# A conditioned attention and feed-forward block: a new written-out order that keeps VectorE and GpSimd apart on their shared port, with a rearranged prologue and filler products

## The chip, the cores and the metric

The kernel runs on one core of a Trainium2 chip. The metric is device time in microseconds, the median of several executions. A profiled execution has a span of its own, from the first to the last instruction. Engines: TensorE (PE), VectorE (DVE), ScalarE (ACT), GpSimd (POOL), and SyncE (SP), which here only issues DMAs.

## The reference

Cut to what matters. There are 2048 tokens of width 448, 16 heads of 28, and 4 segments of 512 tokens. Everything is bf16 in DRAM.

```python
sa, ca, ga, sb, cb, gb = (silu(c) @ w_mod) split in six        # vectors 0..5
h = layernorm(x) * (1 + ca) + sa
x = x + ga * A(h)                  # A: attention with a memory
h = layernorm(x) * (1 + cb) + sb
x = x + gb * (sigmoid(h @ w_gate) * (h @ w_up)) @ w_down

# A, per segment s, per head; q, k, v = h @ wq, h @ wk, h @ wv
a_dot = softmax(q k^T * scale + causal mask) @ v
a_mem = (phi(q) @ M) / (phi(q) @ z + 1e-6)      # phi(t) = t + 1 if t > 0 else exp(t)
o = g * a_mem + (1 - g) * a_dot                 # g = sigmoid(beta)
M += phi(k)^T v ; z += sum phi(k)               # carried to the next segment
A = concat(o) @ wo
```

## The kernel before

The work is tiled by segment (512 tokens, four tiles of 128 rows) and, in attention, by group of four heads (`hc`, four groups). Each segment goes through these stages:

- First norm (`ln1`, statistics L522 and L523 on DVE, reciprocal root L529 and L530 on POOL, `xn` L535 on DVE). For segment 0, TensorE transposes `xn` (L583), and DVE and ACT read the product from PSUM, scaled and shifted by vectors 0 and 1 (L594, L591). For the other segments a DMA transposes `xn` into `hT` (L545), and DVE and ACT scale and shift it in place (L558, L555).
- Projections (`proj`): q and k for each head group (L615, copied out by ACT at L623), v for each token tile (L636, copied at L640). The weights wq and wk are loaded into the buffer of `wd_sb` and copied into padded tiles (L448, L450).
- Attention for each head group: logits in three groups of key blocks (L695, four heads at once), exp on ACT (L704), causal mask on POOL (L710), the product with v (L718), transposition back (L725), normalization and gates (L741, L742, L756; from segment 1 on also the memory's part, L732, L762 and L764 on POOL), transposition again (L766, `oT`).
- Memory (`memory`): phi of k (L647 ACT, L648 and L650 DVE), a DMA transpose (L658), a product with v (L664), and the update (L671, L673, L677). phi of q goes the same way for L732.
- `wo_ln2`: the output product (L779), the residual (L783), the second norm (the same lines as the first), DMA transposes, modulation by vectors 3 and 4.
- `ffn`: fourteen chunks of 128 of the hidden width, each a gate and an up product (L799), tanh (L804), and a combination on DVE (L809); then the down product in three parts of its chunks (L822), the residual (L828), and the store (L830).

Vectors 2 and 5 are not applied to activations. POOL multiplies them into the weights: wo (four instructions, L506) and wd (fourteen, L508). Vectors come from products of silu(c) with w_mod, as columns (L417, read out at L426 and L424) or spread over all partitions (L434, L437). The w_mod columns of vectors 2, 3 and 4, and 5 are three loads into the feed-forward's `fT` buffers. Twenty products on zeros warm TensorE at the start (L836).

The order of all instructions is written out by a list scheduler in the program (class `Graph`): each piece of work is a node with an engine, a duration in ns, its predecessors, and a priority. The scheduler keeps a clock per engine, gives each engine the ready node of highest rank plus priority, hands out PSUM banks and ring buffers, and then emits the instructions in the order it found. It decides the order only; on the chip each engine runs its queue in order and waits on semaphores. `PRM` holds the priorities, and `pace` the earliest times of the head groups' logits:

```python
PRM = dict(T0=10000, STEP0=500.0, STEP=9700.0, lg=95000, ex=-30000, mask=127000, wo=9000, tanh=53500, up=85000,
           f=89500, dn=-507800, phi=8000, t=22000, ln1=-55000, mem=-86000, pj=-6000, ot=331000)
...
def pace(i):
    return PRM["T0"] + PRM["STEP0"] * min(i, NHC) + PRM["STEP"] * max(i - NHC, 0)
```

In this scheduler, DVE and POOL have separate clocks with no link between them, and a load may be issued once the modelled DMA queue is less than `BACKLOG` ns deep.

Of the kernel before, what the change touches and what calls it, by code (L numbers as in the profile page):

```python
# [9 lines left out]
U32 = mybir.dt.uint32  # L10
# [3 lines left out]
P = 128  # L14
# [3 lines left out]
BACKLOG = 1500  # L18


PRM = dict(T0=10000, STEP0=500.0, STEP=9700.0, lg=95000, ex=-30000, mask=127000, wo=9000, tanh=53500, up=85000,
           f=89500, dn=-507800, phi=8000, t=22000, ln1=-55000, mem=-86000, pj=-6000, ot=331000)
# [9 lines left out]
class Node:  # L32
    def __init__(self, eng, dur, fn, deps, take, use, lag, prio, release, mode, move):
        self.eng, self.dur, self.fn = eng, dur, fn
        self.deps = [d for d in deps if d is not None]
        self.take, self.use, self.lag, self.prio, self.release, self.mode = take, use, lag, prio, release, mode
        self.move = move
        self.start = self.end = None
        self.outs = []


class Graph:
# [15 lines left out]
    def add(self, eng, dur, fn, deps=(), take=(), use=(), lag=0, prio=0, release=0, mode=None, move=None):  # L58
        n = Node(eng, dur, fn, deps, take, use, lag, prio, release, mode, move)
# [7 lines left out]
    def ready_at(self, n):  # L67
        t = n.release
        if n.move is not None and n.move > 300:
            t = max(t, self.ring - BACKLOG)  # L70
# [9 lines left out]
    def place(self, n, t, narrow):  # L80

        got = []
        for s in n.take:
# [6 lines left out]
            else:  # L90
                c = [i for i, f in enumerate(free) if f <= t and (s, i) not in got]
# [9 lines left out]
                got.append(c[0])  # L101
        return got

    def run(self):
# [9 lines left out]
        self.ring = 0.0  # L114
        order, t, done = [], 0.0, 0
        while done < len(self.nodes):
            moved = False
            for e in ENGINES:
# [4 lines left out]
                for n in ready:  # L123
                    got = self.place(n, t, narrow)
# [5 lines left out]
                    for s, i in zip(n.take, got):  # L130
                        s.at = i
# [6 lines left out]
                    n.start = t  # L138
                    n.end = t + n.dur + extra
                    at[e] = n.end  # L140
                    if n.move is not None:
                        self.ring = max(self.ring, n.end) + n.move
                        n.lag = self.ring - n.end + LAND
                    avail[e].remove(n)
                    order.append(n)
                    done += 1
                    for s in {id(x): x for x in (*n.take, *n.use)}.values():
                        if all(u.end is not None for u in s.users):
                            f = max(u.end + (u.lag if u.move is not None else 0) for u in s.users) + 120
                            for w in range(s.width):  # L150
                                self.free[s.pool][s.at + w] = f
                    for o in n.outs:
# [8 lines left out]
            times += [r for e in ENGINES for n in avail[e] if (r := self.ready_at(n)) > t]  # L161
            times += [f for fs in self.free.values() for f in fs if t < f < float("inf")]
            assert times, "the graph cannot go on"
            t = min(times)
        for n in order:
            if n.fn is not None:
                n.fn()
        self.order = order
        Graph.last = self
# [3 lines left out]
def kernel(  # L173
# [35 lines left out]
    NWARM = 20  # L209
# [78 lines left out]
    BIG = 1e7  # L288

    def load(eng, dst, src, size, deps=(), prio=0, use=(), take=(), rate=230.0):  # L290
# [5 lines left out]
    l_c = load("SP", c_col[:], c.rearrange("o (p k) -> p (o k)", p=CP), 20000, prio=2 * BIG)  # L296
# [10 lines left out]
    def load_wm(engs, j0, nj, flat, prio, deps=()):  # L307
# [3 lines left out]
                   CP * h * nj * D * 2, prio=prio, deps=deps, rate=230.0 if nj == 1 else 300.0)  # L311
# [5 lines left out]
    def load_w(engs, dst, w, prio, deps=(), cuts=(0, 3)):  # L317

        n = w.shape[1]
        rate = 230.0 if n == D else 380.0  # L320
        a = w[0:3 * P, :].rearrange("(k p) n -> p k n", p=P)
        got = {}
        for i, (k0, k1) in enumerate(zip(cuts, cuts[1:])):
            x = load(engs[i], dst[:, k0:k1, :], a[:, k0:k1, :], (k1 - k0) * P * n * 2, prio=prio - i, deps=deps,
                     rate=rate)
            got.update((k, x) for k in range(k0, k1))
        got[3] = load(engs[-1], dst[0:KR, 3, :], w[3 * P:D, :], KR * n * 2, prio=prio - len(cuts), deps=deps, rate=rate)
# [3 lines left out]
    load_x("SP", 0, 1, 2 * BIG - 100)  # L331
    load_x("ACT", 1, 2, 2 * BIG - 100)
    load_x("SP", 2, 3, 2 * BIG - 200)
    load_x("ACT", 3, 4, 2 * BIG - 200)
    load_wm(("SP", "ACT"), 0, 2, pT_r[:].rearrange("p n h w -> p (n h w)"), 2 * BIG - 300)
    lq = load_w(("SP", "ACT", "ACT"), wq_st, A_wq, 2 * BIG - 400, cuts=(0, 2, 3))
    lk = load_w(("SP", "ACT", "ACT"), wk_st, A_wk, 2 * BIG - 500, cuts=(0, 2, 3))
    lv = load_w(("SP", "SP"), wv_sb, A_wv, BIG - 60)


# [15 lines left out]
    def pads_fn():  # L356
# [4 lines left out]
        nc.vector.memset(wv_sb[KR:P, 3, :], 0.0)  # L361

    n_wz = dve(200, lambda: nc.vector.memset(M_sb[:, 0:2, :], 0.0), prio=BIG)
    n_ident = pool_op(700, ident_fn, prio=BIG)
    n_pads = dve(1800, pads_fn, prio=BIG - 1)
# [4 lines left out]
    n_vpad = [pool_op(700, lambda i=i: vpad_fn(i), prio=BIG - 5) for i in range(NV)]  # L370
    n_wopad = pool_op(1500, lambda: nc.gpsimd.memset(wo_sb[:], 0.0), prio=BIG - 4)

    def gpad_fn():
        nc.gpsimd.memset(wg_sb[KR:P, 3, :], 0.0)
        nc.gpsimd.memset(wu_sb[KR:P, 3, :], 0.0)
        nc.gpsimd.memset(O_r[:, :, :, Dh:HP, :], 0.0)
    n_gpad = pool_op(3500, gpad_fn, prio=0, release=16000)


# [19 lines left out]
    n_bmask = dve(700, bmask2_fn, [pool_op(1700, bmask_fn, release=17000)])  # L399


    def silu_fn():
        nc.vector.tensor_scalar(th[:], th[:], 0.5, 0.5, op0=ALU.mult, op1=ALU.add)
        nc.vector.tensor_tensor(silu[:], th[:], c_col[:], ALU.mult)
    n_th = act(200, lambda: nc.scalar.activation(th[:], c_col[:], AF.Tanh, scale=0.5), [l_c], prio=BIG)
    n_silu = dve(400, silu_fn, [n_th], prio=BIG)
    n_sbc = dve(600, lambda: nc.vector.tensor_copy(
        silu_bc[:], silu[:].rearrange("p (k o) -> p k o", o=1).to_broadcast([CP, NK, P])), [n_silu])
    ROWS = (P, P, P, KR)

    def mod_cols(j, vi, prio):
# [15 lines left out]
        return n, dve(220, ev, [n], use=[b], prio=prio)  # L427
# [12 lines left out]
    mm1, n_ca = mod_cols(1, 1, BIG - 1)  # L440

    def padded(st, dst, loads, eng, prio):
        ns = []
        for k in range(NK):
            def fn(k=k, r=ROWS[k]):
# [3 lines left out]
                else:  # L449
                    (nc.vector if eng[k] == "DVE" else nc.gpsimd).tensor_copy(d, src)  # L450
            ns.append(add(eng[k], {"ACT": 600, "DVE": 400, "POOL": 1000}[eng[k]], fn, [n_pads, loads[k]],
                          prio=prio))
# [429 lines left out]
```

The softmax here doesn't subtract the row's maximum and nothing guards it: scores larger than these inputs give would overflow.

## Time and profile before

| | |
|---|---|
| time, median of 3 | 270.99 us (269.2 to 271.36) |
| span of the profiled execution | 266.6 us |
| PE, DVE, ACT, POOL busy | 245.8, 190.3, 158.0, 106.2 us |
| mean granted TensorE clock | 0.967 |
| L799, 448 matmuls | 117.5 us |
| L822, 224 matmuls | 45.2 us |
| L704, 48 exps | 76.6 us |
| L710, 64 masks | 42.2 us |
| L535, 32 of xn | 17.0 us (mean 568 ns) |
| L508, 14 scalings of wd | 15.3 us |
| HBM read, written | 10.67, 1.84 MB |

A busy time is the union of an engine's instructions. Matmuls overlap, so the mean duration of one (387 ns for 512 columns) is longer than the time from one to the next; the latter is read from the chain that ended last, or from the timeline. DMA rows give the time from the issue to the landing. A line number in a row is the line of the program.

### The profile page before, as it was taken

Reading aid. Unit: us, or ns where it says so; the run is one execution under the profiler, and the core shown is the slowest. Engines: PE = TensorE matmul, PEld = TensorE weight load, DVE = VectorE, ACT = ScalarE, POOL = GpSimd, SP = SyncE. Lnnn points to the kernel's source line nnn. Section 1 sums busy time; section 2 is a strip of 40 time slices with the busy share of each in tenths; the row PEclk is TensorE's granted clock in tenths of the full one; section 3 lists DMA queues with packets and bytes.
Section 4 is the critical chain, followed back from the end, with each engine's and each line's share of the span. In section 5 each row is a group of like instructions: output and inputs, shape, how many; then the busy total and the mean of one; then the engine's idle time right before and its main releaser. Section 6 shows DMA issues by size and latency. Waiting matters only on the chain.

```text
span 266.6 us, 4442 instructions
## 1 busy us (share of the span) xinstructions
PE 245.8 (92%) x1608; PEld 110.0 (41%) x1608; DVE 190.3 (71%) x392; ACT 158.0 (59%) x201; POOL 106.2 (40%) x168
## 2 busy tenths in 40 slices
PE   5799797788984999999999999999999999999994
PEld 1434333243331444444444444443444444444442
DVE  7679748839999999999968896488567833342334
ACT  0559898989885687986987564558521230331010
POOL 8648832447696564562434553006502300000000
PEclk9979899899996899999999999999999999999999
DMA  5999998761051010014011003000000131000103
GB/s 156 305 202 148 298 294 194 197 85 47 0 82 39 1 22 20 0 22 98 1 22 38 20 17 72 6 20 0 2 0 0 31 52 52 0 2 1 52 0 103
DMA packets 33245, 18.03 MB, mean 68 GB/s; under 512 B 22856, under 2 KB 32328, under 8 KB 33224
## 3 DMA queue, kind: packets, MB, share of 16 engines
q1 hardware_dynamic: 32248, 16.78, 29.1%
q10 hardware_dynamic: 976, 0.98, 1.4%
q8 instruction: 12, 0.20, 0.3%
q14 instruction: 9, 0.07, 0.1%
HBM read 10.67 MB, written 1.84 MB: 47 GB/s over the span
## 4 chain that ended last, share of the span: by engine, by line
PE 64%; DVE 3%; issue 1%; ACT 1%; DMA 1%; DVEq 0%
PE ps L799 37%; PE ps L822 15%; PE ps L779 4%; PE ps L695 3%; PE ps L615 2%; PE ps L718 2%; PE ps L732 1%; DVE ot L828 1%; DVE e L648 1%; ACT pT L704 1%; PE ps L664 1%; DMA out_dram<-ot 1%; DVE pq L650 1%; DVE hT L558 0%; DVE fT L809 0%
## 5 line engine op out<-in xcount | busy, mean ns | idle before, releaser
L704 ACT ACTIVATE pT<-ps 128x2048 bf16<-128x2048 f32 (+1 forms) x48 | 76.6, 1596 | 14.5 <-PE ps L695 13.6
L804 ACT ACTIVATE tt<-ps 128x512 f32<-128x512 f32 x56 | 33.4, 597 | 64.0 <-PE ps L799 62.6
L710 POOL TENSOR_SCALAR_AFFINE_SELECT pT<-pT 128x512 bf16<-128x512 bf16 x64 | 42.2, 673 | 60.9 <-ACT pT L704 60.7
L799 PE MATMUL ps<-hT,wg_sb 128*128 128x512 bf16 x224 | 59.0, 387 | 4.1 <-DVE hT L558 4.0
L809 DVE SCALAR_TENSOR_TENSOR fT<-tt,ps 128x512 bf16<-128x512 f32 x56 | 38.0, 682 | 32.2 <-PE ps L799 30.5
L799 PE MATMUL ps<-hT,wu_sb 128*128 128x512 bf16 x224 | 58.5, 384 | 0.0
L822 PE MATMUL ps<-wd_sb,fT 128*128 128x448 bf16 x224 | 45.2, 353 | 0.0
L799 PEld LDWEIGHTS <-wg_sb 128*128 128x128 bf16 x224 | 21.9, 99 | 30.6 <-DVE hT L558 4.3
L799 PEld LDWEIGHTS <-wu_sb 128*128 128x128 bf16 x224 | 21.1, 99 | 26.2 <-issue 2.6
L822 PEld LDWEIGHTS <-fT 128*128 128x128 bf16 x224 | 21.5, 98 | 20.0 <-issue 0.4
L522 DVE BATCH_NORM_STATS2 st<-x_sb 128x6 f32<-128x448 bf16 x32 | 19.5, 609 | 5.4 <-DMA x_sb<-in_A_x_dram 5.3
L764 POOL TENSOR_TENSOR O<-U 128x448 bf16<-128x448 f32 x12 | 13.8, 1150 | 21.2 <-DVE U L762 21.2
L695 PE MATMUL ps<-qT,kT 28*128 28x512 bf16 (+3 forms) x256 | 17.5, 306 | 3.7 <-ACT pT L704 3.1
L828 DVE TENSOR_TENSOR ot<-ps,x_sb 128x448 bf16<-128x448 f32 x16 | 9.9, 619 | 14.4 <-PE ps L822 13.0
L725 DVE STREAM_TRANSPOSE A<-ps 128x512 f32<-128x512 f32 x28 | 18.5, 691 | 1.8 <-PE ps L718 1.6
L615 PE MATMUL ps<-hT,wq_sb 128*128 128x512 bf16 x64 | 19.1, 427 | 0.3 <-DVE hT L594 0.3
L535 DVE TENSOR_SCALAR xn<-x_sb,mv,rs 128x448 bf16<-128x448 bf16 x32 | 17.0, 568 | 2.5 <-POOL rs L530 2.4
L615 PE MATMUL ps<-hT,wk_sb 128*128 128x512 bf16 x64 | 17.7, 402 | 0.0
L530 POOL TENSOR_TENSOR rs<-rs,mhalf 128x1 f32<-128x1 f32 (+1 forms) x23 | 15.2, 662 | 1.9
L650 DVE TENSOR_TENSOR pq<-e 128x512 bf16<-128x512 bf16 x24 | 14.3, 603 | 1.6 <-DVE e L648 0.5
L508 POOL TENSOR_TENSOR wd_sb<-wd_sb,rep 128x448 bf16<-128x448 bf16 x14 | 15.3, 1115 | 0.0
L779 PE MATMUL ps<-wo_sb,oT 128*128 128x448 bf16 x64 | 13.5, 353 | 1.4 <-DVE x_sb L783 1.4
(93 smaller groups left out, 261.8 us busy)
## 6 DMA issues: line engine op xcount, KB each, us to landing
out_dram<-ot SPq DMA_DIRECT2D x16, 112.0 KB, 1.7
x_sb<-in_A_x_dram SPq DMA_DIRECT2D x3, 448.0 KB, 7.1
wg_sb<-in_B_w_gate_dram SPq DMA_DIRECT2D x3, 448.0 KB, 6.2
wu_sb<-in_B_w_up_dram SPq DMA_DIRECT2D x3, 448.0 KB, 7.4
wd_sb<-in_B_w_down_dram SPq DMA_DIRECT2D x2, 448.0 KB
fT<-in_w_mod_dram SPq DMA_DIRECT2D x2, 392.0 KB, 7.3
fT<-in_w_mod_dram SPq DMA_DIRECT2D x1, 784.0 KB, 12.4
wd_sb<-in_B_w_down_dram SPq DMA_DIRECT2D x2, 336.0 KB
```

The source lines that it names most:

```text
L522: nc.vector.bn_stats(st_r[:, st.at, :], src)
L535: n = dve(330, lambda t=t, src=src, xn=xn: nc.vector.tensor_scalar(xn_r[:, xn.at, 0:D], src, mv_r[:, mv.at, t, 0:1], rs_r[:, mv.at, t:t + ...
L615: nc.tensor.matmul(pf(b), lhsT=w_sb[:, kc, hc * 4:(hc + 1) * 4, :].rearrange("p h e -> p (h e)"), rhs=hT_r[:, hT.at, kc, :], start=(kc == ...
L695: nc.tensor.matmul(ps[:, lg.at + hs, o:o + nq], lhsT=kT_r[r, k.at, hc, kb * P:(kb + 1) * P], rhs=qT_r[r, q.at, hc, kb * P:L], start=True, ...
L704: nc.scalar.activation(pT_r[:, pT.at, :, w0:w0 + wid], ps[:, lg.at:lg.at + 4, 0:wid], AF.Exp, scale=scale)
L710: nc.gpsimd.affine_select(out=blk, in_=blk, compare_op=ALU.is_ge, fill=0.0, base=0, pattern=[[0, 4], [1, P]], channel_multiplier=-1)
L725: nc.vector.transpose(A_r[:, A.at, i, :, :].rearrange("p b e -> p (b e)"), pf(b))
L779: nc.tensor.matmul(pf(b)[:, 0:D], lhsT=oT_r[:, oT.at, k, :].rearrange("p (q j) -> p j q", j=2)[:, t // 2, (t % 2) * P:(t % 2 + 1) * P], rh ...
L799: nc.tensor.matmul(pf(b), lhsT=w_sb[:, k, fs], rhs=hT_r[:, hT.at, k, :], start=(k == 0), stop=(k == NK - 1))
L804: a = act(500, lambda gp=gp, tt=tt: nc.scalar.activation(tt_r[:, tt.at, :], pf(gp), AF.Tanh, scale=0.5), [n1], use=[gp, tt], prio=PRM["tanh"])
L809: f = dve(605, lambda up=up, tt=tt, ft=ft: nc.vector.scalar_tensor_tensor(fT_r[:, ft.at, :], tt_r[:, tt.at, :], 1.0, pf(up), op0=ALU.add, ...
L822: nc.tensor.matmul(pf(b)[:, 0:D], lhsT=fT_r[:, fts[fc].at, t * P:(t + 1) * P], rhs=wd_sb[:, fc, :], start=(fc == 0), stop=(fc == NFC - 1))
```

## The change

The change aims at a shorter prologue and at fewer collisions between DVE and POOL.

1. The scheduler gets a common clock, `port`, for DVE and POOL work that is marked with `lock`: a marked node may not end before the port is free plus its own marked time, and if that would stall it for more than `PRM["stall"]` = 300 ns, other work is picked. Marked are the masks, xn, the in-place modulation on DVE, phi on DVE, the memory update's L677, the gate and normalization work, the weight scalings, and POOL's copies and several memsets. Durations are set lower for marked DVE work.
2. Loads: at most eight DMAs in flight instead of `BACKLOG`; other rates. w_mod's vectors 2 to 5 come in one load. wq and wk go through SP only. `c` comes first.
3. Segment 1's norm is turned on TensorE like segment 0's.
4. Prologue: an ACT operation of its own loads the function table early; the warm-up has 12 products; the head gates' operations and masks' constants come later; memsets of wo, wg and wu run as 32-bit words of half the number; the pads of `hT` are set once.
5. One of the fourteen wd scalings goes to DVE (`wdd=1`).
6. `fill`: after the order is found, dummy products on zeros or on `wq_sb` are put into TensorE's planned waits of more than 450 ns before 90 us, into a PSUM bank that is free there.
7. `PRM` has new values throughout.

In the order that results, eight dummies on zeros stand around the first transposes, and nine on `wq_sb` (three, one and five) between there and the first feed-forward product.

```diff
-BACKLOG = 1500
+LANES = 8
+FILL = 450
+PRM = dict(T0=5000, STEP0=500.0, STEP=10100.0, lg=69000, ex=40000, mask=-2000, wo=48000, tanh=24500, up=77000,
+           f=131500, dn=-486800, phi=-10000, t=8000, ln1_1=4000, ln1_2=-72000, ln1_3=-52000, mem=3000,
+           pj_0=3000, pj_1=-19000, pj_2=-15000, pj_3=37000, ot=399000, stall=300, wds=-22000, wos=145000,
+           wdd=1, mod=27000, a0=-62000, w0=3000)
...
+                    if n.lock is not None and self.port - t - n.lock > PRM["stall"]:
+                        continue
...
+                    if n.lock is not None:
+                        extra = max(0.0, self.port - t - n.lock)
                     n.end = t + n.dur + extra
+                    if n.lock is not None:
+                        self.port = n.end
...
+    def fill(self, until, fill):
+        pe = [n for n in self.order if n.eng == "PE"]
+        for a, b in zip(pe, pe[1:]):
+            one = 432 if a.end < 8000 else 216
+            n = int((b.start - a.end - FILL) / one)
+            if n <= 0 or a.end > until:
+                continue
...
-    NWARM = 20
+    NWARM = 12
...
-    lq = load_w(("SP", "ACT", "ACT"), wq_st, A_wq, 2 * BIG - 400, cuts=(0, 2, 3))
-    lk = load_w(("SP", "ACT", "ACT"), wk_st, A_wk, 2 * BIG - 500, cuts=(0, 2, 3))
+    lq = load_w(("SP",) * 3, wq_st, A_wq, 2 * BIG - 400 * MEG, cuts=(0, 2, 3))
+    lk = load_w(("SP",) * 3, wk_st, A_wk, 2 * BIG - 500 * MEG, cuts=(0, 2, 3))
...
+    n_act = act(1400, lambda: nc.scalar.activation(th[:], th[:], AF.Tanh), [n_th0], prio=2 * BIG - 350 * MEG)
...
-    n_wopad = pool_op(1500, lambda: nc.gpsimd.memset(wo_sb[:], 0.0), prio=BIG - 4)
+    n_wopad = pool_op(1000, lambda: nc.gpsimd.memset(wo_sb[:].rearrange("p c n -> p (c n)").bitcast(U32), 0),
+                      prio=BIG - 4 * MEG)
...
-    load_wm(("SP",), 2, 1, fT_flat[:, 2 * NK * D:], lp - 2)
+    load_wm(("SP",), 2, 4, fT_flat, lp - MEG * 2)
...
-    load_wm(("SP",), 3, 2, fT_flat, lp - 6)
...
-    load_wm(("SP",), 5, 1, fT_flat[:, 3 * NK * D:], 0)
...
-    n_coef = dve(1000, coef2_fn, [n_cf, n_hsel])
+    n_coef = dve(1000, coef2_fn, [n_cf, n_hsel], release=14000, lock=0)
...
+            (nc.gpsimd if on_pool else nc.vector).tensor_tensor(wd_sb[:, k, :], wd_sb[:, k, :], rep[:, 1, :], ALU.mult)
...
-        if s == 0:
-            ns = [layer_norms([x_sb[:, t, :]], [xl[t]], BIG - 2)[0] for t in range(TPS)]
+        if s < 2:
+            top = BIG - 2 * MEG if s == 0 else PRM["ln1_1"]
...
-                masks.append(pool_op(640, mask, [e], prio=PRM["mask"], use=[pT]))
+                masks.append(pool_op(610, mask, [e], prio=PRM["mask"] + a0, use=[pT], lock=0))
...
+    def dummy(i, n, at):
+        for _ in range(n):
+            if at < 12000:
+                nc.tensor.matmul(ps[:, i, :], lhsT=wz[:, 0:P], rhs=wz, start=True, stop=True)
+            else:
+                w = wq_sb[:, 0, :, :].rearrange("p h e -> p (h e)")
+                nc.tensor.matmul(ps[:, i, :], lhsT=w[:, 0:P], rhs=w, start=True, stop=True)
+    G.fill(90000, dummy)
+    G.emit()
```

## The prediction

> **What bounds the kernel now.** I read the busy slices of the page first, then the table of engine time by stretch, the chain that ended last, and the timeline of the stretches where TensorE waits. The slices place the loss: TensorE is full from the fourteenth slice on (90 us), and only before that are there holes and granted clocks below full. The windows put numbers to it.
>
> ```profile
> PE   5799797788984999999999999999999999999994
> DVE  7679748839999999999968896488567833342334
> ACT  0559898989885687986987564558521230331010
> PEclk9979899899996899999999999999999999999999
> ...
> 31.00:63.00 32.00, 27.75 (x205) 11.79 (x205) 21.01 (x53) 29.18 (x39) 14.13 (x20) 0.90 0.84 192
> 63.00:84.20 21.20, 14.65 (x111) 6.09 (x112) 20.75 (x35) 17.79 (x23) 18.19 (x25) 0.95 0.21 32
> 84.20:98.10 13.90, 13.83 (x88) 5.46 (x89) 13.11 (x23) 9.23 (x12) 8.58 (x10) 0.83 0.09 19
> 98.10:263.00 164.90, 164.88 (x1018) 74.98 (x1017) 111.21 (x219) 83.42 (x102) 42.84 (x69) 1.00 0.10 24
> ```
>
> The columns of a window are PE, weight load, DVE, ACT, POOL, clock, DMA share, GB/s. From 98.1 us the bound is TensorE (164.88 of 164.90). From 31 to 63 it is ACT (29.18 of 32). From 63 to 84.2 it is DVE (20.75 of 21.2), which shares that stretch with a POOL busy for 18.19. So the kernel is a prologue that ends when the first feed-forward product starts (L799, at 84.17), and behind it a TensorE queue that never drains. The timeline shows what ends the prologue:
>
> ```profile
> 78.89 1.86 DVE L648 TENSOR_SCALAR e<-kT 128x512 bf16<-128x512 bf16 x2
> 80.56 3.41 POOL L508 TENSOR_TENSOR wd_sb<-wd_sb,rep 128x448 bf16<-128x448 bf16 x3
> 80.67 2.41 DVE L650 TENSOR_TENSOR pq<-e 128x512 bf16<-128x512 bf16 x2
> 83.00 1.75 DVE L558 TENSOR_SCALAR hT<-hT,cols 128x512 bf16<-128x512 bf16 x2
> 84.17 1.03 PE L799 MATMUL ps<-hT,wg_sb 128*128 128x512 bf16 x2 [3.99 <-DVE hT L558]
> ```
>
> The DVE operations stretch beside POOL's: two of L648 take 1.86 us and two of L650 2.41, where one of each takes 0.25 and 0.43 at 53.44 and 53.78, with POOL idle as they start. They stand ahead of L558, for which TensorE waits. And the first matmuls after the wait are slow: the chain has L799 x12 in 5.03 us (0.419 each) at 84.17, and x68 in 14.78 (0.217 each) at 159.31.
>
> **What the Trainium skill says.** "SBUF — State Buffer", Who interferes with whom: GpSimd's port pair is also VectorE's second pair, taken exclusively for a whole instruction; tensor_scalar, copy and cast in 2-port modes take it, and two SBUF inputs contend with GpSimd's reads. The trace agrees: L535 (xn) is 0.35 us alone and four took 4.33 us at 18.20, beside the memsets L374 and L375 (1.59 and 1.71). "TensorE: Matmul & The Clock Gate", What's actually happening: the clock halves after about 3.4 us of idling and is full again after as much work. The trace agrees: 0.419 against 0.217 after a wait of 3.99 us. The same page, Part 4: PE-mode transpose, says a 128x128 transpose takes about 275 ns and does not warm the clock; here L583 is 220 ns long, sixteen take about 1.1 us of issue (0.068 each), and the projections behind them did start at 0.43 each.
>
> **The yardstick.** I count the TensorE work ordered behind the first feed-forward product, at the chain's durations: L799 448 x 0.216 = 96.7, L822 224 x 0.1885 = 42.2, L779 48 x 0.1885 = 9.1, L615 28 x 0.216 = 6.0, logits 7.5 (0.22 for four, 0.33 for eight), L718 6.4, L732 3.0, L664 1.8: 172.7 us. The new order holds the same 448, 224, 48 and 28 behind its first feed-forward product: 172.7 too. Measured, before: 10.8 of it stands in 84.2 to 98.1, which took 13.9 (3.1 lost, 2.4 of it the slow clock: 5.03 - 12 x 0.217); 161.8 takes 164.9 (3.1 for changes of tile shape, such as 0.97 where four of L799 take 0.86 elsewhere). After the last matmul at 263.0 come 3.6 us of output. So span = F + L + 175.8 + 3.6, with F the start of the first feed-forward product and L the loss just behind it: 84.2 + 3.1 + 175.8 + 3.6 = 266.7, against 266.6. The change is worth what it does to F and L.
>
> **The change, part by part.**
> *Prologue.* Before, w_mod's first half on SP was issued at 3.43, eighth in line, and its products started at 9.24; they ended at 10.6, but the columns (L426) were read at 12.40, behind five operations on the head gates (L494 to L499). Now it is fourth in line, about 1.2 us earlier, and the gate operations go behind segment 1. Products at 8.0, columns at 9.7, projections at about 11.2 instead of 13.38. All of wq and wk now goes through SP; 1.66 MB to the end of wq, at the 300 GB/s of the busy slices, is there by 9 to 10, so it does not hold this up by more than a microsecond. Dummies and the earlier start of the warm-up (its memset is second on DVE, not eighth) keep the clock up: sixteen matmuls at 0.216 = 3.5 us, where 13.38 to 18.62 was used. First exp: 11.2 + 3.5 + 0.8 = 15.5, against 19.21. Bounds 14.5 to 18.
> *Segment 1 on TensorE.* Removed: four DMA transposes (6.10 us on SP) and the pass over hT that waited for them (L558 at 28.6, projections at 31.76 after 2.00 us of idling). Added: 16 transposes, 1.1 us of TensorE, and the 0.54 and 0.77 us reads of L594 and L591 in place of L558 and L555 (0.41 and 0.81). Chain: stats by 15, rstd by 16.7, xn by 18.3, transposes by 19.5, ACT's share behind the third exp at about 23.5, projections at 24. TensorE has no other work it needs there; but the transposes stand ahead of the third logits, so a late x tile would hold ACT. x of segment 1 is 2.9 MB into the loads, about 13 us.
> *One load for vectors 2 to 5, and the queue.* 1.6 MB now goes ahead of wo and x of segment 2; x of segment 3 is 7.5 MB into the loads, 28 us at 300 GB/s, and DVE's statistics for it stand before the first PV transposition (30.87 before). I take no cost; bound 0 to 8 us. The first DMA transpose of segment 2 now stands behind all weights (10.7 MB, 37 us); its projections are ordered behind the third PV, at about 47. Hidden.
> *Port order and priorities.* ACT's work from the first exp to the sixth head group's last exp is 52.1 us before and 53.1 after, counted at pitches of the timeline (1.77 and 0.92 for exps, 0.47, 0.43, 0.53 and 0.72 for the rest); before it took 59.1 (19.21 to 78.26), 7.0 idle. The two ACT passes over hT for the first feed-forward (1.4) come next. Idle will shrink, not vanish, since segment 1 comes earlier and DVE is less blocked: I take 4.5 (bounds 1 and 7). That gives 15.5 + 53.1 + 4.5 + 1.4 = 74.5, and the sixth PV, with its mask (0.64) and 0.66, stands before L845 too: F = 75.5. The DVE side allows it: from the last oT of segment 0 (ACT's twelfth exp at about 53, plus 5, hence 58), ordered DVE work to the last xn is 9.3 us undisturbed, then a transpose of 2.5 and 0.8 of modulation, 13 us; with 20% of blocking, 15.5: 73.5. Before it took 20.7.
> *Fillers.* Nine in the prologue's later part (1.9 us of TensorE) lie in waits. With shorter waits before F, L falls from 3.1 to 0.8 (bounds 0 and 3.1).
> *Smaller memsets* (32-bit, half the elements) halve about 5 us of POOL, all beside other work. One of fourteen scalings of wd goes to DVE: 0.3 to 0.5 us, hidden, needed 30 us after F.
>
> Sum: 75.5 + 0.8 + 175.8 + 3.6 = 255.7, which is 10.9 under 266.6. Median: 270.99 - 10.9 = 260.1.
>
> **The rivals.** (A) The blocking only moves: POOL's 18.19 and DVE's 20.75 in 63 to 84.2 are the same operations, so F keeps all 7 us of ACT idling and the clock loss, and only the start's gain remains with 1 us of the rest: about 266. For: DVE has no slack there; against: 4 us of it is stretched time. (B) ACT runs nearly without idling (1 us) and the clock stays up: F = 71.5, L = 0, 250.9, hence about 255.3. For: ACT already runs at 29.18 of 32; against: each exp still waits for a bank half and masks. (C) Slower: loads in front of DVE's statistics and the late transposes hold the first heads. If x of segment 3 lands as late as it did (DVE waited until 40.99), the first head's PV transposition slips by 10 us, two pT buffers fill, ACT stops, and F = 87: 270.99 + 3 = 274. For: DVE executes in order; against: it is 7.5 MB deep, and 300 GB/s was seen.
>
> **Numbers.** Forecast 0.68, A 0.15, B 0.09, C 0.08. Time 260.1. Range 254.5 to 266.5: the ends are B a little beyond and A; C and half of A's upper side are out. Faster by over 1% 0.88, within 1% 0.06, slower 0.06.
>
> **What would show it.** First exp at 15 to 16; segment 1's projections near 24 with no DMA transpose before; L648, L650 and L558 near 0.25, 0.43 and 0.41 between 50 and 75; first feed-forward product at 74 to 77, at 0.216 each; about 180 us from there to the end (182.4 before). It is wrong if that product starts after 80, if DVE waits for x beyond 31, or if TensorE shows idling after F.

## The result and the profile after

The changed kernel takes 259.9 us (median of four runs, 259.13 to 260.64); the kernel before took 270.1 beside it. The ratio is 0.962, with a 95% interval of 0.956 to 0.968. The forecast was 260.1, and the range from 254.5 to 266.5. An execution more than 1.5% above the fastest of its kernel counts as slow and is left out of the ratios, which below takes out one of four for e3_no_fill, two of four for e6_no_lock and three of twenty for e12_before_lock.

The page and the windows of the changed kernel, in the same columns as before (PE, weight load, DVE, ACT, POOL, clock, DMA share, GB/s). Its lines have new numbers: logits L740, exp L749, feed-forward products L845, in-place modulation L599 (DVE) and L596 (ACT), phi L692 and L694, xn L576, wd scalings L548.

```profile
PE   8897599999999999999999999999999999999994
DVE  7574596838986699996988669886458773433403
ACT  2578669999999877496986586377523102233200
PEclk9799869999999999999999999999999999999999
...
31.00:63.00 32.00, 29.25 (x229) 12.39 (x229) 23.44 (x68) 28.29 (x36) 12.75 (x17) 0.91 0.56 113
63.00:76.00 13.00, 12.94 (x90) 5.59 (x89) 12.51 (x26) 12.61 (x20) 11.88 (x18) 1.00 0.30 48
76.00:90.00 14.00, 13.79 (x102) 5.59 (x104) 9.11 (x19) 13.26 (x17) 11.52 (x15) 1.00 0.12 24
90.00:255.00 165.00, 164.56 (x1034) 74.92 (x1031) 114.08 (x228) 83.20 (x102) 48.13 (x73) 1.00 0.10 24
```

The last hole is now in the fifth slice (26 to 32 us). From 63 us on TensorE is full at full clock, while DVE and POOL still share that stretch; where the kernel before left TensorE idle for 6.6 us between 63 and 84.2, this one has next to nothing. The timeline at the end of the prologue:

```profile
70.69 2.04 POOL L548 TENSOR_TENSOR wd_sb<-wd_sb,rep 128x448 bf16<-128x448 bf16 x2
71.89 0.89 DVE L787 TENSOR_TENSOR R<-R,coef 128x32 f32<-128x32 f32 x1
76.10 0.69 DVE L599 TENSOR_SCALAR hT<-hT,cols 128x512 bf16<-128x512 bf16 x2
76.43 1.54 ACT L596 ACTIVATE hT<-hT,cols 128x512 bf16<-128x512 bf16 x2
77.30 2.08 POOL L548 TENSOR_TENSOR wd_sb<-wd_sb,rep 128x448 bf16<-128x448 bf16 x2
77.60 0.89 DVE L692 TENSOR_SCALAR e<-kT 128x512 bf16<-128x512 bf16 x1
77.88 1.04 PE L845 MATMUL ps<-hT,wg_sb 128*128 128x512 bf16 x4
78.75 1.03 PE L845 MATMUL ps<-hT,wu_sb 128*128 128x512 bf16 x4
```

The modulation for which TensorE waited takes 0.69 us for two (1.75 before), with no scaling beside it: two scalings stand 3.4 us ahead of it (and still stretch L787), the next two behind it. The first product starts at 77.88 (84.17 before), waits for nothing to speak of, and runs at 0.217 each. The groups of DVE (columns: count, busy time and mean ns, idle time before them), first of the kernel before, then of the changed one:

```profile
L648 DVE TENSOR_SCALAR e<-qT 128x512 bf16<-128x512 bf16 x12 | 6.3, 522 | 0.0
L558 DVE TENSOR_SCALAR hT<-hT,cols 128x512 bf16<-128x512 bf16 x14 | 8.8, 656 | 7.6 <-DMA hT<-xn 7.6
L650 DVE TENSOR_TENSOR pq<-e 128x512 bf16<-128x512 bf16 x24 | 14.3, 603 | 1.6 <-DVE e L648 0.5
```

```profile
L692 DVE TENSOR_SCALAR e<-qT 128x512 bf16<-128x512 bf16 x12 | 5.0, 418 | 0.0
L599 DVE TENSOR_SCALAR hT<-hT,cols 128x512 bf16<-128x512 bf16 x12 | 4.4, 399 | 2.0 <-DMA hT<-xn 2.0
L694 DVE TENSOR_TENSOR pq<-e 128x512 bf16<-128x512 bf16 x24 | 14.0, 585 | 1.0
```

So DVE is not generally free of POOL: L694 is stretched as before (0.585 against 0.43 alone). What has come free is the in-place modulation (0.656 to 0.399, 14 of them before and 12 after), which a product waits for. The two halves of the run, up to the first feed-forward product and from there to the end, before and after:

```profile
0.00:84.17 84.17, 66.91 (x502) 29.57 (x503) 65.13 (x151) 65.33 (x87) 54.74 (x90) 0.93 0.75 161
84.17:266.60 182.43, 178.87 (x1106) 80.47 (x1106) 125.17 (x242) 92.65 (x114) 51.45 (x79) 0.99 0.10 25
```

```profile
0.00:77.88 77.88, 69.37 (x530) 31.54 (x531) 55.85 (x153) 62.62 (x88) 44.77 (x83) 0.93 0.68 167
77.88:258.20 180.32, 176.68 (x1111) 79.84 (x1103) 122.29 (x242) 94.58 (x116) 58.16 (x85) 1.00 0.11 25
```

In this pair of profiles 6.3 us come from the first half and 2.1 from the second. Their sum, 8.4, is less than the 10.2 between the medians, because the profiled execution of the kernel before took 268.65 us, below its median of 270.1, while that of the changed kernel took 260.01, close to its own. Within the first half, the first exp comes 2.3 earlier (16.87 against 19.21), but the twelfth (the end of segment 0's attention) ends at 57.04 against 57.43. That would mean that the earlier start is given back, but one pair of profiles does not show it: in e1 and e2 below, which keep the order of before up to that point, the twelfth ends at 59.88 and 60.67, and in e8, with the changed order, at 57.79. From the twelfth exp to the first feed-forward product it is 20.8 us instead of 26.7.

### The profile page after: what moved, and what is told of

The parts are those of the page before. It is cut to its first block, busy times and chain, and to the rows that moved or that the text cites. A ratio compares the mean times of both kernels' runs of the same rounds, so it can differ in the third digit from the quotient of the medians.

```text
span 258.2 us, 4484 instructions
## 1 busy us (share of the span) xinstructions
PE 246.0 (95%) x1633; PEld 111.4 (43%) x1633; DVE 178.1 (69%) x394; ACT 157.2 (61%) x202; POOL 102.9 (40%) x167
## 4 chain that ended last, share of the span: by engine, by line
PE 77%; DMA 13%; ACT 4%; DVE 2%; SPq 1%; issue 1%; DVEq 0%; ACTq 0%
PE ps L845 38%; PE ps L868 16%; PE ps L659 7%; PE ps L825 5%; PE ps L740 4%; DMA fT<-in_w_mod_dram 4%; DMA x_sb<-in_A_x_dram 4%; PE ps L763 4%; ACT pT L749 2%; DMA wd_sb<-in_A_wq_dram 2%; DMA hT<-xn 2%; PE ps L680 2%; SPq L328 1%; PE ps L777 1%; PE ps L708 1%; DMA pk<-pq 1%
## 5 line engine op out<-in xcount | busy, mean ns | idle before, releaser
L749 ACT ACTIVATE pT<-ps 128x2048 bf16<-128x2048 f32 (+1 forms) x48 | 77.0, 1605 | 18.3 <-PE ps L740 15.4
L755 POOL TENSOR_SCALAR_AFFINE_SELECT pT<-pT 128x512 bf16<-128x512 bf16 x64 | 43.5, 692 | 58.5 <-ACT pT L749 58.4
L845 PE MATMUL ps<-hT,wg_sb 128*128 128x512 bf16 x224 | 57.6, 380 | 0.0
L845 PE MATMUL ps<-hT,wu_sb 128*128 128x512 bf16 x224 | 57.5, 379 | 0.0
L845 PEld LDWEIGHTS <-wu_sb 128*128 128x128 bf16 x224 | 21.8, 98 | 26.3
L845 PEld LDWEIGHTS <-wg_sb 128*128 128x128 bf16 x224 | 20.7, 98 | 24.9 <-issue 2.1
L868 PEld LDWEIGHTS <-fT 128*128 128x128 bf16 x224 | 21.3, 98 | 20.4 <-issue 1.2
L874 DVE TENSOR_TENSOR ot<-ps,x_sb 128x448 bf16<-128x448 f32 x16 | 9.9, 619 | 16.7 <-PE ps L868 15.7
L740 PE MATMUL ps<-qT,kT 28*128 28x512 bf16 (+3 forms) x256 | 17.5, 306 | 4.0 <-DVE cols L463 2.9
L659 PE MATMUL ps<-hT,wq_sb 128*128 128x512 bf16 x64 | 17.5, 399 | 0.0
L659 PE MATMUL ps<-hT,wk_sb 128*128 128x512 bf16 x64 | 17.1, 391 | 0.0
L596 ACT ACTIVATE hT<-hT,cols 128x512 bf16<-128x512 bf16 (+1 forms) x12 | 9.5, 830 | 11.0 <-DMA hT<-xn 10.9
L576 DVE TENSOR_SCALAR xn<-x_sb,mv,rs 128x448 bf16<-128x448 bf16 x32 | 14.2, 482 | 1.9 <-POOL rs L571 1.9
L740 PEld LDWEIGHTS <-kT 28*128 28x128 bf16 x256 | 5.6, 92 | 21.4 <-issue 20.6
L694 DVE TENSOR_TENSOR pq<-e 128x512 bf16<-128x512 bf16 x24 | 14.0, 585 | 1.0
```

Source lines behind the costliest of these rows:

```text
L576: n = dve(300, lambda t=t, src=src, xn=xn: nc.vector.tensor_scalar(xn_r[:, xn.at, 0:D], src, mv_r[:, mv.at, t, 0:1], rs_r[:, mv.at, t:t + ...
L659: nc.tensor.matmul(pf(b), lhsT=w_sb[:, kc, hc * 4:(hc + 1) * 4, :].rearrange("p h e -> p (h e)"), rhs=hT_r[:, hT.at, kc, :], start=(kc == ...
L740: nc.tensor.matmul(ps[:, lg.at + hs, o:o + nq], lhsT=kT_r[r, k.at, hc, kb * P:(kb + 1) * P], rhs=qT_r[r, q.at, hc, kb * P:L], start=True, ...
L749: nc.scalar.activation(pT_r[:, pT.at, :, w0:w0 + wid], ps[:, lg.at:lg.at + 4, 0:wid], AF.Exp, scale=scale)
L755: nc.gpsimd.affine_select(out=blk, in_=blk, compare_op=ALU.is_ge, fill=0.0, base=0, pattern=[[0, 4], [1, P]], channel_multiplier=-1)
L845: nc.tensor.matmul(pf(b), lhsT=w_sb[:, k, fs], rhs=hT_r[:, hT.at, k, :], start=(k == 0), stop=(k == NK - 1))
```

## The experiments

Twelve kernels ran. In the table, F is the start of the first feed-forward product in the profile; the ratio is to the kernel before, run beside each.

| run | ratio, 95% interval | span | 12th exp ends | F | F to end |
|---|---|---|---|---|---|
| before | 1 | 266.6 | 57.43 | 84.17 | 182.4 |
| after | 0.962 (0.956 to 0.968) | 258.2 | 57.04 | 77.88 | 180.3 |
| e1_hT_first | 1.001 (0.998 to 1.003) | 267.8 | 59.88 | 81.88 | 185.9 |
| e2_no_wd | 0.980 (0.975 to 0.985) | 263.0 | 60.67 | 81.06 | 181.9 |
| e3_no_fill | 0.965 (0.958 to 0.973) | 256.9 | 55.54 | 76.64 | 180.3 |
| e4_x3_first | 0.957 (0.953 to 0.962) | 257.5 | 56.21 | 77.21 | 180.3 |
| e5_x2x3_first | 0.965 (0.958 to 0.972) | 257.3 | 56.01 | 77.03 | 180.3 |
| e6_no_lock | 0.990 (0.981 to 0.998) | 264.5 | 55.44 | 77.64 | 186.9 |
| e7_seg1_dma | 1.010 (1.004 to 1.017) | 271.1 | 57.53 | 87.95 | 183.2 |
| e8_after_no_wd | 0.959 (0.954 to 0.965) | 258.8 | 57.79 | 78.87 | 179.9 |
| e10_stats_behind | 0.960 (0.957 to 0.964) | 257.1 | 55.63 | 76.80 | 180.3 |
| e11_stats_no_fill | 0.963 (0.959 to 0.966) | 258.6 | 55.25 | 77.15 | 181.5 |
| e12_before_lock | 0.999 (0.997 to 1.002) | 266.6 | 55.07 | 77.00 | 189.6 |
| e13_no_lock_no_wd | 0.983 (0.979 to 0.988) | 263.9 | 55.89 | 76.02 | 187.9 |

The theory: DVE is blocked by POOL's scalings just where TensorE waits, and the new order takes the scalings from there. The rivals: it is the place of the modulation in DVE's queue, not the scalings; it is the fillers and the clock; it is the prologue. No run takes the prologue's changes out of the changed kernel, so the last rival is not tested by itself.

### Is it the scalings, or DVE's order?

e1_hT_first changes the order of the kernel before in one place: the two modulations of segment 0's second norm go ahead of four phi operations.

```diff
+        for k, n in enumerate(early):        # the two L558 nodes of segment 0's second norm
+            order.remove(n)
+            order.insert(at + k, n)          # at: four DVE nodes earlier
```

> The kernel before, with one edit of the order found: the two VectorE modulations of the first feed-forward's input (L558 of segment 0's second norm) stand ahead of the four phi(k) operations that stood in front of them. Theory 'order' (much of the gain from the last oT of segment 0 to the first feed-forward product comes from what stands in VectorE's queue there, and needs no model of the port): the input's DMA transposes land at about 79.4, so the first product starts at 80.5 to 81 instead of 84.2, and the span falls by 3 to 4 us. Rival 'port' (the modulation stretches beside GpSimd wherever it stands): the start moves by less than 1.5 us.

The product came earlier (81.88), and nothing was won. The phi operations now stand behind the modulation and stretch beside the same scalings, and the PSUM read that TensorE needs next stands behind them. The timeline of e1_hT_first, where L519 are the scalings, L659 is phi, L736 the transposition back from PSUM, and L813 the products:

```profile
81.64 3.15 POOL L519 TENSOR_TENSOR wd_sb<-wd_sb,rep 128x448 bf16<-128x448 bf16 x3
82.78 2.15 DVE L659 TENSOR_SCALAR e<-kT 128x512 bf16<-128x512 bf16 x2
86.72 0.59 PE L813 MATMUL ps<-hT,wu_sb 128*128 128x512 bf16 x1 [3.21 <-DVE A L736]
```

The wait of 3.99 us has become one of 3.21 behind the product. Order alone in this one place does not do it.

e2_no_wd leaves the fourteen scalings out of the kernel before, so the feed-forward part is not scaled by its vector; the order stays.

```diff
-    W_d = [pool_op(1050, lambda k=k: nc.gpsimd.tensor_tensor(wd_sb[:, k, :], wd_sb[:, k, :], rep[:, 1, :], ALU.mult),
+    W_d = [pool_op(1050, lambda k=k: None,
```

> The kernel before, with GpSimd's fourteen multiplications of wd by vector 5 left out (the down product then uses the weights unscaled); order unchanged. Theory 'port': VectorE's operations between 61 and 84 us lose the 4 to 5 us by which they stretched beside these instructions, and the first feed-forward product starts at 79 to 80 instead of 84.2; span 4 to 5 us shorter. Rival 'order': the operations in front of the modulation still run one after another and the start moves by less than 1.5 us.

It gains 5.5 us (0.0203 x 270; 4.2 to 6.8 by the interval), and from the twelfth exp to the product it is 20.4 us, as in the changed kernel (20.8). The modulation itself is still stretched there, beside a mask and a sum on POOL (1.56 us for two, at 80.28). What has become short is DVE's work ahead of it: the two L648 of k take 0.49 instead of 1.86, and the two L650 behind them 1.63 instead of 2.41.

e8_after_no_wd makes the same cut in the changed kernel.

```diff
         def wd_fn(k=k, on_pool=on_pool):
-            (nc.gpsimd if on_pool else nc.vector).tensor_tensor(wd_sb[:, k, :], wd_sb[:, k, :], rep[:, 1, :], ALU.mult)
+            pass
```

> The changed kernel without GpSimd's 14 scalings of the down weights (left out: the output's feed-forward part is not scaled by its vector); the order otherwise as it is. It measures how much of the blocking that these scalings cause is left. Theory (the new order has moved them out of VectorE's way): less than 1.5 us faster than the changed kernel, where the same cut was worth 5 us in the kernel before. Rival (the blocking is as large as before and the gain came from elsewhere): 4 to 6 us faster than the changed kernel, ratio .94 to .946.

Here it is worth 0.8 us (0.0028 x 270), with intervals that overlap, although 14 us of POOL and 2.3 us of DVE's busy time went (178.1 to 175.8, of which 0.6 is the one scaling that DVE had). So the change has taken the scalings off the path: what cost about 5.5 us before costs 0.8 now, which can't be told from nothing.

The same two runs say how much of the gain that is. With the scalings left out of both kernels, the new order is still 5.5 us faster (0.980 against 0.959, intervals far apart), so the scalings explain 4.7 of the 10.2 us, about half. In these two profiles the other half lies ahead of the twelfth exp (57.79 against 60.67, though equal orders differ by up to 3.2 us there) and behind F (179.9 against 181.9), not between them. Which of the other changes brings it (prologue, loads, priorities, other marked operations) is not shown.

### Is it the planner's clock for the port?

e6_no_lock runs the changed planner with the marks ignored; e13_no_lock_no_wd takes the scalings out of that order too (unscaled, as above); e12_before_lock gives the kernel before that clock, with the two shorter durations of phi; the weight copies at the start stay unmarked, and the other durations and all priorities stay as they were. All three are planned anew.

```diff
-        self.move, self.lock = move, lock
+        self.move, self.lock = move, None
```

> The changed kernel with its planner run without the clock of the shared port (an operation of GpSimd and one of VectorE may overlap in the plan at no cost); durations, priorities, fillers and the rest as they are; the order is planned anew from it. Theory (the order that takes the port for exclusive brings the gain between the twelfth exponential and the first feed-forward product): VectorE's in-place multiplications and the second norms are stretched again, the first feed-forward product comes 2 to 5 us later than 77.9, the ratio is .97 to .98. Rival (priorities, the wider memset and TensorE's norm carry the gain): within 1 us of the changed kernel.

> The changed kernel planned without the clock of the port (its order as in the run of that name, ratio .990) and without the 14 scalings of the down weights, which are left out, so that the feed-forward part is not scaled. If the 9.7 us that this order loses against the changed kernel are the scalings' blocking: ratio .957 to .967, as the changed kernel. If they come from priorities that were meant for another plan: within 2 us of that run, ratio .983 to .992. Half and half in between.

> The kernel before with one part of the change alone: its planner gets the clock of the shared port (GpSimd's masks, scalings, sums and the set-up of two buffers against VectorE's in-place multiplications and sums, with the changed kernel's rule and its two shorter durations for phi); priorities, prologue and loads as before; planned anew. If the port order carries the gain: 3 to 6 us faster than before, ratio .978 to .989. If it needs the priorities and the prologue that came with it: within 2 us of before either way, ratio .993 to 1.008.

e6 loses 7.4 us against the changed kernel (0.0275 x 270; its four executions spread from 266.4 to 274.0), but not in the way that the theory said: its F is 77.64, as early as in the changed kernel. The loss stands behind F (186.9 against 180.3). By the windows, TensorE does 507 matmuls ahead of F where the changed kernel does 530, with 29 dummies in both. Behind F it is then busy 3.1 us longer (179.8) and idle 3.4 us longer (7.1). Two of the waits, one on each side of F, from the timeline of e6_no_lock:

```profile
72.32 1.02 PE L659 MATMUL ps<-hT,wk_sb 128*128 128x512 bf16 x4 [1.61 <-DVE A L770]
134.44 1.02 PE L845 MATMUL ps<-hT,wg_sb 128*128 128x512 bf16 x4 [1.97 <-DVE M_sb L717]
```

Taking the scalings out of it (e13) brings 1.7 us of the 7.4 (0.0063 x 270, intervals overlapping; the 9.7 in its expectation is the difference of the medians of all executions). So most of what this order loses is not the scalings' blocking. The waits above say that this order leaves TensorE short of work at other times; whether POOL's masks and sums have a part in that was not tested. And the clock alone, in the kernel before (e12), brings nothing, with F at 77.00: seven microseconds earlier than before, all lost behind it. The timeline and the two halves of e12_before_lock:

```profile
72.71 0.40 PE L702 MATMUL ps<-qT,kT 28*128 28x512 bf16 x4 [1.67 <-ACT pT L711]
75.14 0.62 PE L702 MATMUL ps<-qT,kT 28*128 28x384 bf16 x8 [1.38 <-ACT pT L711]
77.00 2.05 PE L806 MATMUL ps<-hT,wg_sb 128*128 128x512 bf16 x4 [1.24 <-DVE hT L565]
...
0.00:77.00 77.00, 61.60 (x484) 27.12 (x491) 53.78 (x144) 61.74 (x82) 44.56 (x82) 0.89 0.78 174
77.00:266.60 189.60, 182.06 (x1102) 82.14 (x1118) 129.35 (x249) 96.14 (x120) 61.51 (x87) 0.99 0.10 24
```

By the weight loads, 491 stand ahead of F, where the kernel before has 503. Behind F TensorE is busy for 3.2 us more than there (182.06 against 178.87), part of it at half clock (2.05 us for the first four products), and idle for 4.0 more. So an early F is worth nothing if it is reached by leaving work for later, or by an order that starves TensorE behind it. Before and after do nearly the same work behind F: 1106 and 1103 weight loads. How much of the gain is the port's clock and how much the priorities that were set together with it can't be told from these runs: the clock alone gives nothing, and the priorities without it keep a gain of 2.8 us (0.0104 x 270).

### Segment 1's norm on TensorE

e7_seg1_dma turns segment 1 by the DMA queue again, planned anew.

```diff
-        if s < 2:
+        if s < 1:
```

> The changed kernel with the norm of segment 1 turned by the DMA queue again, as before the change; planned anew. Theory (the turn on TensorE takes segment 1's normed tiles off the queue that serves segments 2 and 3 too): the projections of segment 1 come later and the first feed-forward product 1 to 4 us later than 77.9, ratio .965 to .975. Rival (the turn on TensorE buys nothing, since the projections of segment 1 stood at 33.85 us in the changed kernel, later than the 31.76 of the kernel before): within 1 us of the changed kernel, ratio .957 to .967.

It is 13 us slower than the changed kernel (0.0481 x 270), far beyond either expectation. The timeline of e7_seg1_dma just ahead of F:

```profile
79.74 0.29 PE L740 MATMUL ps<-qT,kT 28*128 28x256 bf16 x4 [2.37 <-ACT pT L749]
84.31 3.49 PE L906 MATMUL ps<-wq_sb 128*128 128x512 bf16 x8
87.95 1.04 PE L845 MATMUL ps<-hT,wg_sb 128*128 128x512 bf16 x4
```

The planner put other things first: all of the next segment's projections (57.8 to 67.5) ahead of segment 0's output products, which start at 70.35 instead of 61.65, and 39 filler products of 12.4 us (L906) instead of 9 of 2.5, some at half clock, as the 3.49 us for eight. What the turn on TensorE is worth by itself is therefore not measured; these priorities were chosen together with it.

### The fillers

e3_no_fill leaves the 17 fillers out of the changed kernel; they compute nothing that is used.

```diff
-    G.fill(90000, dummy)
```

> The changed kernel without the seventeen filler products, order otherwise unchanged. Theory 'waits are short' (the clock stays up before the first feed-forward product [...]): the loss behind that product stays at about 0.9 us, the first projections start 0.6 us earlier but run at 0.43 us each [...]; span 0 to 1 us longer. Rival 'fillers' (they are what took the loss from 3.1 to 0.9): the first feed-forward products run at 0.42 again, span 2 to 3 us longer.

No difference that the intervals show, and the first feed-forward products still at full rate (four in 1.04 at 76.64). The profiled span, 1.3 us shorter than the changed kernel's, is the lowest of four; the others are 260.1 to 261.6. e11_stats_no_fill, below, has no fillers either, and there the clock did fall. The timeline of e11_stats_no_fill, and two windows in the same columns as above, in which the granted clock goes from 1.00 to 0.50:

```profile
73.09 1.26 PE L740 MATMUL ps<-qT,kT 28*128 28x256 bf16 x8
75.75 0.40 PE L708 MATMUL ps<-vt,pk 128*128 128x128 bf16 x4 [1.39 <-DMA pk<-pq]
76.07 1.14 PE L763 MATMUL ps<-pT,vt 128*32 128x512 bf16 x16
77.15 1.89 PE L845 MATMUL ps<-hT,wg_sb 128*128 128x512 bf16 x4
...
73.00:76.00 3.00, 1.36 (x13) 0.57 (x12) 2.49 (x4) 3.00 (x6) 2.60 (x4) 1.00 0.44 87
76.30:79.60 3.30, 3.30 (x22) 1.22 (x15) 2.10 (x5) 3.19 (x4) 2.93 (x4) 0.50 0.02 4
```

The fall costs 1.2 us from F to the end (181.5 against 180.3). In the changed kernel five fillers stand in that gap (75.11, 1.25 us). So in this run they would have saved about 1 us. At the start, four of them run on zeros between the transposes and the first projections (1.91 us at half clock at 10.82). Together they bring nothing that can be measured.

### The loads in front of the statistics

The changed kernel waits for x of segment 3. Its timeline (DVE's statistics wait for the load; the read-out of vector 3 stands behind them; TensorE needs that bank; the fifth exp waits for TensorE):

```profile
30.38 0.63 DVE L563 BATCH_NORM_STATS2 st<-x_sb 128x6 f32<-128x448 bf16 x1 [2.84 <-DMA x_sb<-in_A_x_dram]
32.12 0.62 PE L740 MATMUL ps<-qT,kT 28*128 28x384 bf16 x8 [2.92 <-DVE cols L463]
32.78 1.88 ACT L749 ACTIVATE pT<-ps 128x2048 bf16<-128x2048 f32 x1 [2.55 <-PE ps L740]
```

e4_x3_first loads x of segment 3 ahead of wg; e5_x2x3_first loads x of segments 2 and 3 ahead of the one load of vectors 2 to 5; e10_stats_behind leaves the loads and puts the waiting statistics behind the reads that stand ready.

```diff
+    G.order.remove(x3)                                            # e4
+    G.order.insert(G.order.index(lg_[0]), x3)
...
+    for n in (xl[2 * TPS], xl[3 * TPS]):                          # e5
+        G.order.remove(n)
+        G.order.insert(G.order.index(wml[2][0]), n)
...
+    for n, behind in ((s2, dv[i2 + 2]), (s3[0], dv[i3 + 5]), (s3[1], s3[0])):   # e10
+        G.order.remove(n)
+        G.order.insert(G.order.index(behind) + 1, n)
```

> The changed kernel with one edit of the order found: the load of segment 3's x stands ahead of the four loads of w_gate instead of behind them. Theory 'load in front of statistics': VectorE's wait of 2.84 us at 30.4 goes, with TensorE's 2.92 and ScalarE's 2.55 behind it; the fourth head group's last exp ends 1.5 to 2.5 us earlier (57.0 now), the first feed-forward product starts 1 to 2.5 us earlier (77.9 now), span 256 to 257. Rival 'given back': the DMA transposes of segments 2 and 3 land when the last weights have landed, so ScalarE waits there instead, and the span stays within 0.7 us.

> The changed kernel with one edit in the order of the loads alone: x of segments 2 and 3 are loaded ahead of the one load of vectors 2 to 5. Theory (the loads stand in front of VectorE's statistics, and these in front of its PSUM reads): both waits of the statistics (1.94 us until 23.60 and 2.84 us until 30.38) go, the stretch from the first exponential to the end of the twelfth gets 1.5 to 2.5 us shorter, the first feed-forward product comes at 75 to 76, the span is 255 to 256.5 us and the ratio .948 to .955. Rival (the vectors and the normed tiles that wait for them come later by as much): within 0.7 us of the changed kernel, ratio .957 to .964.

> The changed kernel with VectorE's order edited in two places and nothing else: the first statistic of segment 2 stands behind segment 1's two PSUM reads, and the first two of segment 3 behind the read-out of vector 3, a normed tile, the gates and the read-out of vector 4. The loads stay where they are. Theory (a statistic that waits for its load costs because PSUM reads stand behind it): the 1.60 us and 2.92 us that TensorE waited at 24.94 and 32.12 shrink to under 0.5 each, the twelfth exponential ends 2 to 4 us earlier than 57.0, the first feed-forward product comes at 74.5 to 76.5, the span is 254.8 to 256.8 us, the ratio .945 to .955. Rival (as when the loads were moved, the time is taken back before the first feed-forward product): within 0.7 us of the changed kernel.

> The same edit of VectorE's order, and the 17 filler products left out (they compute nothing that is used). If the edit works and the four fillers on zeros at 10.82 hold up the first projections, this is the shortest of all: first exponential at 15.8, span 254 to 256 us, ratio .943 to .953. If the missing fillers let TensorE's clock fall, or the time is given back: span 257 to 259 us, ratio .957 to .966.

In all of them the wait at 30.4 is gone or moved, F comes 0.7 to 1.1 us earlier, and the times can't be told from the changed kernel's. In e4 the statistics of segment 2 wait until 24.45 instead, and TensorE waits 3.52 us for what stands behind them. e10 shows what took the place of the two waits (1.60 and 2.92 us):

```profile
32.97 1.02 PE L659 MATMUL ps<-hT,wq_sb 128*128 128x512 bf16 x4 [1.28 <-DVE cols L461]
35.98 1.02 PE L659 MATMUL ps<-hT,wq_sb 128*128 128x512 bf16 x4 [1.12 <-DVE A L770]
41.99 0.87 PE L708 MATMUL ps<-vt,pk 128*128 128x128 bf16 x8 [1.64 <-DMA pk<-pq]
```

The gates' small operations (L529 to L533) now meet POOL's scalings of wo and take 3.0 us (29.56 to 32.53) instead of 0.8; then the memory's DMA transpose is what TensorE waits for. Three waits of 4.0 us stand for two of 4.5. No version was found that is told apart from the changed kernel as faster: e4 (0.957) and e10 (0.960) have the lowest ratios, and both intervals overlap with its own.

## Why the prediction was right, step by step

**The sum.** Span = F + L + 175.8 + 3.6 was to be 255.7 with F = 75.5 and L = 0.8. It was 258.2, with F = 77.88 and, by subtraction, L = 0.9. So the span was missed by 2.5 us, and that the time was met to 0.2 is luck: the forecast takes its 10.9 us from a median of 270.99, while the span of 266.6 that it starts from belongs to an execution of 268.65. The yardstick held for this order: from F to the end it is 180.3 in five of the seven kernels that keep it (179.9 in e8, 181.5 in e11). It does not hold for orders planned anew (183 to 190): e6, e12 and e13 leave more for behind F (1118 to 1126 weight loads instead of 1103), and e7, which leaves less, waits more there. It held here because the counts of work behind F were taken from the new order itself.

**First exp: 15.5 predicted, 16.87 measured.** With the same order of the start, the runs had 15.3 to 17.4 us. It was 15.3 to 15.8 where the sixteen transposes took 1.07 us (e4, e6, e8), and 15.8 to 17.4 where they took 1.46 to 1.89: TensorE's clock was down (granted 0.50 from 9.6 to 12.9 in the changed kernel, 1.00 from 6 to 16 in e4, e6 and e8). The prediction took the warm-up to hold it. The Trainium skill, "TensorE: Matmul & The Clock Gate", Part 1, What's actually happening, says that the window in which activity is judged runs free, so that the point at which the clock changes differs from run to run; these runs agree with that, though none isolates it. And the step mattered less than its place in the sum says. F does not follow the first exp: 15.66 goes with 78.87 (e8), 17.28 with 76.80 (e10).

**x of segment 3: cost taken as 0, measured 2.9 us of waiting.** It is the wait above, at 30.38, just below the 31 that was named as a sign of being wrong. Within the bounds of 0 to 8, but not hidden. What it costs at the end is about 1 us of span in single profiles (e5, e10), which the times do not confirm.

**Segment 1: projections at 24 predicted, 33.85 measured.** The transposes came at 22.0 to 25.3, not by 19.5; the projections stand behind logits that waited for the read-out above.

**ACT's idling: 4.5 predicted, 6.7 measured** (first exp to the end of the eighteenth, 59.8, less 53.1 of work). With the loads out of the way it is 5.1 (e5: 58.25 less 53.1) and 4.8 (e10). So F = 75.5 missed by 2.4: 1.4 too little in the first exp, 2.2 in the idling, and 1.2 too much in the last step, since F came 1.25 us after the eighteenth exp's end and not 2.4.

**DVE's side: 13 to 15.5 predicted, 16.7 measured** from segment 0's last oT (61.19) to F. The blocking did not go away: between 71.9 and 75.8, beside a scaling, a mask and a sum on POOL, L787, L692 and L694 take 0.89, 0.72 and 1.18, where 0.19, 0.25 and 0.43 are seen undisturbed. That L648, L650 and L558 would be near 0.25, 0.43 and 0.41 between 50 and 75 came true for the last one only (0.412; the other two 0.27 to 0.49, and 0.61).

**L: size right, cause half wrong.** It was credited to fillers and shorter waits. Without fillers it was 0.9 once (e3) and 2.1 once (e11). The shorter wait (3.99 us to next to nothing) is the likely cause of most of it; no run separates it. The prediction read the slow products behind the wait of 3.99 us in the kernel before as agreeing with its rule for the clock. The granted clock does not agree: TensorE falls idle at 80.19, and the clock is 1.00 up to 81.9 and 0.50 from 82.0 on, so it fell less than 2 us into the wait.

**The rivals.** A (the blocking only moves) had F stay late. e1 and e12 show a form of it: there F comes earlier and the end does not. It fell for the change since its order keeps the same work behind F as before and lets TensorE run through it: next to no waiting behind F beside the 3.6 of output (180.32 less 176.68), with the scalings away from what it waits for. B needed ACT to idle 1 us, and it idled 6.7. C needed x of segment 3 as late as 40.99, and it came at 30.38. F itself lies 0.9 outside the 74 to 77 that was to be seen.

## What to carry to other kernels

Where a long in-order queue of one engine sets the end, an earlier start of its last stage counts only with the work done ahead of it: look at what is left behind that point and at the waits there (a start at 77.0 gained nothing, one at 77.9 gained 10 us). To learn what a collision costs, leave the disturbing operations out in both kernels: here 5.5 us before and 0.8 after, though some of the disturbed operations stayed as long as they were. The difference between the two kernels without them (5.5 us) is what the collision does not explain. And here an order that was tuned with a model lost more when one term of the model was taken away (7.4 us) than that term brought when it was added alone (0).

## What the runs showed of the hardware

TensorE's clock fell without a long wait: in e11 a single wait of 1.39 us among short products (busy 1.36 of the 3 us from 73 to 76) was followed by a granted clock of 0.50 and products at 0.42 instead of 0.217, while in e3 a wait of 1.04 at the same place (busy 1.71) was not. By the Trainium skill, "TensorE: Matmul & The Clock Gate", What's actually happening, it takes about 3.4 us of idling; here less was enough, and the measurement decides.

Tiny operations pay as much as large ones beside POOL's scalings: L529 and L530, on 16 elements per partition, took 1.00 and 0.95 us in e10 at 29.56 and 30.59, and 0.16 and 0.17 undisturbed. The lines of e10:

```profile
29.48 3.02 POOL L541 TENSOR_TENSOR wo_sb<-wo_sb,rep 128x448 bf16<-128x448 bf16 x3
29.56 1.00 DVE L529 TENSOR_SCALAR cft<-coef 128x16 f32<-128x16 f32 x1
30.59 0.95 DVE L530 TENSOR_TENSOR cft<-cft,hsel 128x16 f32<-128x16 f32 x1
31.58 0.17 DVE L532 TENSOR_REDUCE cfc<-cft 128x4 f32<-128x16 f32 x1
31.79 0.74 DVE L533 TENSOR_SCALAR cfc<-cfc 128x4 f32<-128x4 f32 x1
```

L529, L530 and L533 end at 30.56, 31.54 and 32.53; the three scalings, at a third of 3.02 us each, end near 30.5, 31.5 and 32.5. So each of the small operations lasted until the scaling beside it was over, while the reduction between them was not held. That agrees with the Trainium skill, "SBUF — State Buffer", Who interferes with whom, that the port is held for a whole instruction: the wait is set by the other engine's operation (about 1.03 us), not by the size of one's own.
